# Attention in four phases of sixteen scores a group: four scores copied out by DVE before their exponential, v's sums added up in the SBUF, PSUM banks given out anew in every phase

## The chip, the cores and the metric

The kernel runs on one core of one Trainium2 chip. The metric is device time in microseconds (us) of one execution, as the median of several. One execution is profiled; where a stage is spoken of, its times are counted from the start of the profiled span.

## What is computed

The input x has 2048 tokens of 512 channels. The result mixes a softmax attention with 32 heads of 16 channels and a token-mixing MLP by a gate for each token:

```
qkv    = x @ wqkv                                  # 32 heads, Dh = 16
scores = einsum("bhqd,bhkd->bhqk", q, k) * Dh**-0.5
a      = (softmax(scores) @ v) @ wo
u      = gelu(einsum("bsd,sf->bdf", layernorm(x), w1) + b1)
b      = transpose(einsum("bdf,fs->bds", u, w2) + b2)
out    = g * a + (1 - g) * b                       # g = sigmoid((x * gate_w).sum(-1))
```

## The kernel before

Before the stage that is changed, q, k and v are projected, the layer norm and the first MLP layer are done, and the parts of q and k lie in DRAM (`qp`, `kp`). The changed stage is a hand-written order for all engines: 32 groups (`NG`), each of two heads and one half of the 2048 queries. A group has 64 scores. A score (L806) is one matmul of 128 keys by 512 queries for one head; it uses 64 of the 128 rows of TensorE (`ROWS`, `HALF`), so that it can run beside another matmul of 64 rows. What runs beside the scores is the dense work: the second MLP layer (`second_layer`, tile `dn`) and the output projection (`project`), each matmul done as two halves of 64 rows (L846), the first half in an even phase and the second half in the odd one after it. `put`, `put_outputs` and `sizes_of` write down how many dense matmuls go into which pair of phases (`dense`), and `call` at which pair a transfer is started.

A group runs in eleven phases: ten of six scores and one of four. After the scores of a phase comes `apply_v` for the scores of the phase before: for each score four matmuls (two halves of the queries on two of the four 32-column blocks of TensorE, L770), with 17 columns of v (16 channels and a one, whose product is the softmax's sum). They add up over the whole group in one PSUM bank, `av`.

The PSUM has eight banks: six for scores (`ps_s`, three tiles `s` of two banks), one for `dn`, one for `av`. ScalarE takes two scores in one exponential of 128 x 1024 (L815) from a tile `s` to a tile `pt` in the SBUF, which v's matmuls read.

At the end of a group `evacuate` copies `av` to `ot` (L733), stores the 64 rows of sums (L739, to `o_d`), inverts the softmax's sums on a whole 128 x 512 tile (L743, L744) and stores the inverses a phase later (L749, to `r_d`). Four groups make a block of 128 channels; `fetch_o` brings the block back, with each inverse broadcast over 16 rows (L606, L607), and multiplies and splits it on VectorE (L610, L65, L66: `divide`), when the list `slow` comes to it: at most one such step in an odd phase.

DMAs of this stage are issued by SP in program order: `load_q` of the next group (8 transfers) and `load_k` (6 transfers of 128 KB) at the group's first two phases, the weights of the second layer (L133), stores and fetches between them. A small POOL memset (`token`, L850) orders the two halves of the dense matmuls. After the last group the last block is finished in PSUM (`others`, `last_pair`): the last eight output tiles have then had 8 of their 12 matmuls (`EARLY`).

## Time and profile before

| what | us |
|---|---|
| median of 3 runs | 1308.75 (1307.37 to 1309.79) |
| profiled execution, its span | 1307.9 |
| first stage, to the first exponential | 0 to 304.8 |
| attention, first to last exponential | 304.8 to 1288.2 |
| what follows | 1288.2 to 1307.9 |

The profiled execution's span runs from its first to its last instruction; its own time lies within the runs shown, and the median is 0.85 us above the span. In the lines of the profile below an engine is PE (TensorE's matmuls), PEld (its weight loads), DVE (VectorE), ACT (ScalarE), POOL (GpSimd) or SP (whose queue, SPq, issues DMAs). A row of the timeline has the start, the duration, the engine, the line, the operation and the tiles (out<-in); "x8" are eight of them in a row, and in brackets stands how long the engine was idle before and who released it. A group's row has busy time, mean ns of one, and the idle time before.

### The profile page before, as it was taken

The numbers are of one execution on the slowest core, as the hardware profiler recorded it, in microseconds if no ns is written. First come the engines' busy times: TensorE is split into PE (matmuls) and PEld (weight loads), VectorE is DVE, ScalarE is ACT, GpSimd is POOL, SyncE is SP. The second block draws the span as 40 slices with busy tenths as digits, with TensorE's granted clock in tenths as the row PEclk, the third lists the DMA queues.
The fourth block names the chain that finished last, engine by engine and source line by source line (L and its number), as shares of the span: only waits on it lengthen the run. The fifth ranks groups of instructions, "written<-read, shape, count | busy, mean of one in ns | idle before, by whom it ended". The sixth has DMA issues, their size and how long they took to land.

```text
span 1307.9 us, 32289 instructions
## 1 busy us (share of the span) xinstructions
PE 1299.0 (99%) x13282; PEld 764.0 (58%) x13282; DVE 402.9 (31%) x538; ACT 1090.6 (83%) x1248; POOL 200.9 (15%) x467
## 2 busy tenths in 40 slices
PE   9999999999999999999999999999999999999997
PEld 7888888886555555555555555455555545544444
DVE  5675361445121111122322111232111112233324
ACT  3443343448999999999999999999999999999994
POOL 0210244453101011011100111100010101100000
PEclk9999999999999999999999999999999999999999
DMA  4497643327343334334554343544333333365511
GB/s 129 137 314 274 227 119 98 97 81 154 74 86 66 62 74 84 69 75 92 124 113 120 81 82 73 115 112 118 78 66 62 76 64 78 76 120 120 117 55 69
DMA packets 93384, 138.41 MB, mean 106 GB/s; under 512 B 14293, under 2 KB 53355, under 8 KB 90156
## 3 DMA queue, kind: packets, MB, share of 16 engines
q1 hardware_dynamic: 92652, 135.20, 43.3%
q8 instruction: 107, 1.75, 0.6%
q10 hardware_dynamic: 576, 1.05, 0.2%
q14 instruction: 49, 0.40, 0.1%
HBM read 99.63 MB, written 36.56 MB: 104 GB/s over the span
## 4 chain that ended last, share of the span: by engine, by line
PE 99%; DMA 0%; SPq 0%; DVE 0%; issue 0%
PE av L770 37%; PE s L806 29%; PE acc L414 12%; PE acc L73 10%; PE dn L846 10%; PE pa L889 1%; PE acc L186 1%; PE dn L791 0%; DMA x<-in_A_x_dram 0%; PE acc L253 0%; PE pa L919 0%; SPq L178 0%; DVE base L932 0%; PE pa L897 0%; PE pa L896 0%; SPq L171 0%
## 5 line engine op out<-in xcount | busy, mean ns | idle before, releaser
L815 ACT ACTIVATE pt<-s 128x1024 f32<-128x1024 f32 x1024 | 962.5, 1025 | 20.8 <-PE s L806 13.5
L806 PE MATMUL s<-qs,ks 64*128 64x512 f32 x2048 | 521.2, 420 | 0.0
L770 PE MATMUL av<-pt,v 128*17 128x256 f32 x8192 | 510.6, 381 | 0.0
L806 PEld LDWEIGHTS s<-qs,ks 64*128 64x128 f32 x2048 | 297.6, 184 | 207.7 <-ACT pt L815 183.2
L770 PEld LDWEIGHTS av<-pt,v 128*17 128x17 f32 x8192 | 205.3, 97 | 259.5 <-issue 119.2
L846 PE MATMUL dn<-u_hi,w_hi 64*128 64x512 f32 x428 | 179.7, 420 | 0.0
L846 PE MATMUL dn<-u_lo,w_hi 64*128 64x512 f32 x430 | 170.1, 396 | 0.0
L846 PE MATMUL dn<-u_hi,w_lo 64*128 64x512 f32 x430 | 170.1, 396 | 0.0
L66 POOL TENSOR_TENSOR w_lo<-w_raw,w_hi 128x512 fp32r<-128x512 f32 (+1 forms) x126 | 152.3, 1210 | 115.0 <-ACT w_hi L65 108.4
L850 POOL MEMSET token<- 1x1 f32 x320 | 30.1, 94 | 872.3 <-PE dn L846 695.1
L733 DVE COPY ot<-av 128x512 f32<-128x512 f32 x31 | 21.4, 692 | 347.6 <-PE av L770 347.6
L65 ACT CAST w_hi<-w_raw 128x512 fp32r<-128x512 f32 (+1 forms) x67 | 38.1, 569 | 79.5 <-PE acc L414 58.8
L744 DVE RECIPROCAL rt<-rt 128x512 f32<-128x512 f32 x31 | 104.0, 3353 | 1.1
L414 PE MATMUL acc<-h_hi,w_hi 128*128 128x512 f32 x224 | 87.1, 389 | 0.0
L414 PE MATMUL acc<-h_lo,w_hi 128*128 128x512 f32 x224 | 87.1, 389 | 0.0
L414 PE MATMUL acc<-h_hi,w_lo 128*128 128x512 f32 x224 | 87.1, 389 | 0.0
L65 DVE CAST w_hi<-w_raw 128x512 fp32r<-128x512 f32 (+1 forms) x61 | 23.5, 386 | 190.5 <-PE s L806 82.0
L846 PEld LDWEIGHTS dn<-u_lo,w_hi 64*128 64x128 f32 x430 | 79.5, 185 | 2.5 <-POOL token L850 0.2
L846 PEld LDWEIGHTS dn<-u_hi,w_lo 64*128 64x128 f32 x430 | 79.4, 185 | 2.6
L846 PEld LDWEIGHTS dn<-u_hi,w_hi 64*128 64x128 f32 x428 | 78.8, 184 | 2.2
L73 PE MATMUL acc<-xt_hi,wc_hi 128*128 128x512 f32 x128 | 49.8, 389 | 0.0
L73 PE MATMUL acc<-xt_lo,wc_hi 128*128 128x512 f32 x128 | 49.8, 389 | 0.0
(142 smaller groups left out, 1000.5 us busy)
## 6 DMA issues: line engine op xcount, KB each, us to landing
w_raw<-in_B_w_dram SPq DMA_DIRECT2D x96, 256.0 KB
ks<-kp SPq DMA_DIRECT2D x192, 128.0 KB
qs<-qp SPq DMA_DIRECT2D x256, 64.0 KB
qp<-pc SPq DMA_DIRECT2D x16, 768.0 KB
x<-in_A_x_dram SPq DMA_DIRECT2D x32, 256.0 KB
kp<-pc SPq DMA_DIRECT2D x16, 512.0 KB
w_raw<-in_B_w_dram SPq DMA_DIRECT2D x32, 128.0 KB
bp<-row SPq DMA_DIRECT2D x16, 256.0 KB
```

What stands on the lines that cost most here:

```text
L65: copy(hi, src)
L66: return sub(lo, src, hi.bitcast(F32), ALU.subtract)
L73: nc.tensor.matmul(ps, a, b, start=start and n == 0, stop=stop and n == last)
L186: nc.tensor.transpose(turns[t][:, k, :], xs[t][:, k * P : (k + 1) * P], ident)
L414: nc.tensor.matmul(p, a, b, start=first and k == 0, stop=last and k == 2)
L733: nc.vector.tensor_copy(ot, av)
L744: nc.vector.reciprocal(rt, rt)
L770: nc.tensor.matmul(av[32 * j : 32 * j + VC, i * QC : (i + 1) * QC], v[:, c, g % NP * 2 + i, :], pt[:, h * QC : (h + 1) * QC], start=added[ ...
L806: nc.tensor.matmul(s[:, m, :], kt[grp][rows, c * P : (c + 1) * P], qt[grp][rows, qb * NB : (qb + 1) * NB], start=True, stop=True,)
L815: nc.scalar.activation(pt, s, AF.Exp, scale=SCALE)
L846: mm = nc.tensor.matmul(ps, a[half], b[half], start=first and not second, stop=last and bool(second))
L850: fence = nc.gpsimd.memset(token, 0.0)
```

## The change

A group now runs in four phases of sixteen scores (`PHASES`, `NSC`), 128 phases in all, numbered p. In an even phase 14 dense first halves run beside the scores, in the odd phase after it the 14 second halves. In each phase:

- the scores 1, 3, 5 and 7 are copied by DVE to the SBUF (`EVAC`), and ACT makes one exponential of 128 x 2048 of the four, in place, after all others of the phase (two of 128 x 1024 in the last phase);
- the scores 0, 2, 4, 6, 8 and 9 have an exponential of 128 x 512 each (`SINGLE`), the last six go in pairs (`TWO`; in the first phase of a group the first of these pairs is two single ones);
- seven banks are given out anew (`shares`): scores 0 to 6 take one each, 7 to 9 those of 0 to 2, 10 to 15 those of 3 to 8, and v's matmuls take that of 2 and 9. The bank in which the sums were is the last one that the next phase uses (for its score 6);
- `apply_v` runs in the phase itself, without the four copied scores, which are held back for the next phase (`HELD`). Its sums are closed in every phase, and DVE copies them to `ot` or adds them there. v's weights are 32 columns wide (`v_flat`, of which 17 count). In the first phase of a group the held scores of the group before come first, in a bank of their own, and `store` follows.

`store` writes sums and softmax sums as they are (8 transfers). `invert` fetches the softmax sums of a finished block in the phase after, as a 128 x 64 tile, inverts them and puts them back to `ri_d` in the next one. `fetch_o` has its DVE steps at fixed phases (`on_dve`). The dense work has another order: the second layer first (phases 0 to 91), four phases without dense work, then the output tiles; there is no store and reload of half-made output tiles any more, and of the last eight tiles two have 6 and six have 8 of their 12 matmuls before the end.

```
-    v = v_pool.tile([P, NS, H, VC], F32, name="v")
+    v_flat = v_pool.tile([P, NS * H * VC + HALF], F32, name="v")
+    v = v_flat[:, : NS * H * VC].rearrange("p (t h c) -> p t h c", h=H, c=VC)
...
+        nc.gpsimd.memset(v_flat[:, NS * H * VC :], 0.0)
...
+    PHASES, NSC, BANKS = 4, 16, 7
+    LAST = NG * PHASES - 1
...
+    ri_d = [[dram.tile([P // DH, QW], F32, name=f"ri{h}{k}") for k in range(ND)] for h in range(2)]
...
-    ptp = ptp_ctx.enter_context(tc.tile_pool(name="pt", bufs=6, reuse_waits="tile"))
+    ptp = ptp_ctx.enter_context(tc.tile_pool(name="pt", bufs=2, reuse_waits="tile"))
...
-    ps_s = psum_ctx.enter_context(tc.tile_pool(name="ps_s", bufs=3, space=PSUM, reuse_waits="tile"))
...
-    ps_av = psum_ctx.enter_context(tc.tile_pool(name="ps_av", bufs=1, space=PSUM, reuse_waits="tile"))
...
+    def invert(half, k, pairs, at):
...
+        w = QW // DH
+        t = out_pool.tile([P, w], F32, name="inv")[: n * DH]
+        nc.sync.dma_start(t, r_d[half][k][:n].rearrange("r (a b) -> (r a) b", b=w))
+
+        def turn():
+            nc.vector.tensor_scalar_max(t, t, LEAST_SUM)
+            nc.vector.reciprocal(t, t)
+
+        on_dve(at, turn)
+        def put_back():
+            nc.sync.dma_start(ri_d[half][k][:n].rearrange("r (a b) -> (r a) b", b=w), t)
+
+        calls.setdefault(at + 1, []).insert(0, (put_back,))
...
+    def fetch_o(half, k, places, ats, pairs=4):
...
+        rb = end.tile([P, QW], F32, name="o_sum", bufs=2)[: n * DH]
+        hi, lo = (place(i)[: n * DH] for i in places)
         raw = lo.bitcast(F32)
         nc.sync.dma_start(raw, o_d[half][k][: n * DH])
+        nc.sync.dma_start(rb, ri_d[half][k][:n, None, :].broadcast_to([n, DH, QW]))
+        on_dve(ats[0], nc.vector.tensor_mul, rb, raw, rb)
+        on_dve(ats[1], nc.vector.tensor_copy, hi, rb)
+        on_dve(ats[2], nc.vector.tensor_tensor, lo, rb, hi.bitcast(F32), ALU.subtract)
...
+    def put_output(t, m, at):
+        steps, load = project(t, m)
+        call(2 * at - 2, load)
+        return put(steps, at, [m])
...
+    first, at = steps[:28], put(steps[28:], 0, [14])
+    for t in range(1, NS):
+        at = put(second_layer(t), at, [14] * 3)
+    for half in range(2):
+        for k in range(ND):
+            pairs = 3 if half and k == ND - 1 else 4
+            p0 = PHASES * (half * NP + 4 * k + pairs)
+            call(p0 + 1, invert, half, k, pairs, p0 + 1)
+    p0 = 2 * at
+    call(p0, open_end)
+    call(p0, fetch_o, 0, 0, (0, 1), (p0 + 1, p0 + 1, p0 + 1))
+    call(p0, fetch_o, 0, 1, (2, 3), (p0 + 1, p0 + 2, p0 + 2))
+    call(p0 + 2, fetch_o, 0, 2, (4, 5), (p0 + 2, p0 + 2, p0 + 3))
+    call(p0 + 3, fetch_o, 0, 3, (6, 7), (p0 + 3, p0 + 3, p0 + 3))
+    at += 2
+    for t in range(NH):
+        at = put_output(t, 3 * ND, at)
+    p1 = PHASES * (NP + 2 * 4) + 3
+    call(p1, fetch_o, 1, 0, (8, 9), (p1 + 1, p1 + 2, p1 + 2))
+    call(p1 + 3, fetch_o, 1, 1, (10, 11), (p1 + 4, p1 + 5, p1 + 5))
+    p2 = PHASES * (NP + 3 * 4) + 2
+    assert p2 > 2 * at
+    call(p2, fetch_o, 1, 2, (0, 1), (p2 + 1, p2 + 1, p2 + 1))
+    call(p2 + 4, load_wq, p2 + 4)
+    call(LAST - 1, fetch_o, 1, 3, (2, 3), (LAST, LAST, LAST), 3)
+    for t in range(NH, NS):
+        at = put_output(t, 6 if 2 * at < p2 + 2 else 8, at)
+    assert at == NG * PHASES // 2
...
+    EVAC = 1, 3, 5, 7
+    SINGLE = 0, 2, 4, 6, 8, 9
+    TWO = (10, 11), (12, 13), (14, 15)
+    TURNS = [(0, 2), (4, 6), (8, 9), *TWO]
+    HELD = [(1, 3), (5, 7)]
...
+    def shares(n):
+
+        for one in range(0, BANKS, 2):
+            lows = [k for k in range(one)][::2] + [k for k in range(one + 1, BANKS)][::2]
+            for third in lows:
+                if n in (third, third + 1):
+                    first, second = (low for low in lows if low != third)
+                    return [first, first + 1, one, second, second + 1, 2 * third + 1 - n, n]
+
...
+        for j in range(4):
+            rows, cols = slice(32 * j, 32 * j + VC), slice(j * QC, (j + 1) * QC)
             dst = o_d[half][k][2 * p * DH : 2 * (p + 1) * DH, cols].rearrange("(i r) n -> r i n", i=2)
             nc.sync.dma_start(dst, ot[rows][:DH].rearrange("r (i n) -> r i n", i=2))
-
-        def invert():
-            rt = out_pool.tile([P, NB], F32, name="rt", bufs=1)
-            nc.vector.tensor_scalar_max(rt, ot, LEAST_SUM)
-            nc.vector.reciprocal(rt, rt)
-
-            def store():
-                for rows, cols in blocks:
-                    dst = r_d[half][k][None, 2 * p : 2 * (p + 1), cols]
-                    nc.sync.dma_start(dst, rt[rows][DH:].rearrange("r (i n) -> r i n", i=2))
-
-            stores.append(store)
-
-        slow.insert(0, (two, invert))
-
-    added = [0, 0]
-
-    def pairs_of(g, units, last):
-
-        pairs = list(zip(*([u for u in units if u[2] == qb] for qb in range(2))))
-        return [(g, pair, last and n == len(pairs) - 1) for n, pair in enumerate(pairs)]
-
-    def apply_v(pairs):
-        ot = None
-        for g, pair, last in pairs:
-            for i, c, qb, pt in pair:
-
-                added[qb] += 1
+            dst = r_d[half][k][None, 2 * p : 2 * (p + 1), cols]
+            nc.sync.dma_start(dst, ot[rows][DH:].rearrange("r (i n) -> r i n", i=2))
...
+    def apply_v(av, grp, pairs, final=False):
+
+        for n, pair in enumerate(pairs):
+            for i, c, qb, pt in sorted(pair, key=lambda u: u[2]):
...
+                    v_at = (c * H + grp % NP * 2 + i) * VC
                     nc.tensor.matmul(
-                        av[32 * j : 32 * j + VC, i * QC : (i + 1) * QC],
-                        v[:, c, g % NP * 2 + i, :],
+                        av[32 * j : 32 * (j + 1), i * QC : (i + 1) * QC],
+                        v_flat[:, v_at : v_at + 32],
                         pt[:, h * QC : (h + 1) * QC],
-                        start=added[qb] == 1,
-                        stop=added[qb] == 2 * NS,
+                        start=n == 0,
+                        stop=n == len(pairs) - 1,
...
+        for x, y, more in parts:
+            if more:
+                nc.vector.tensor_tensor(x, y, x, ALU.add)
+            else:
+                nc.vector.tensor_copy(x, y)
+        for n in halves:
+            begun[n] = True
+        if final and grp < NG - 1:
+            store(grp, sums.pop(grp)[0])
...
+        for p in range(LAST + 1):
+            grp, ph = divmod(p, PHASES)
+            second = ph % 2
+            if ph == 0:
+                at = [[0, 0], [0, 0]]
+                if grp + 1 < NG:
                     qt[grp + 1] = load_q(grp + 1)
-                if ph == 1 and grp + 1 < NG:
-                    kt[grp + 1] = load_k(grp + 1)
-                two, second = divmod(ph, 2)
-                two += grp * TWOS
-                if ph == 2 * TWOS:
-                    n_s, beside = 4, []
-                elif second:
-                    n_s = 6
+            if ph == 1 and grp + 1 < NG:
+                kt[grp + 1] = load_k(grp + 1)
+            for what, *args in calls.get(p, ()):
+                what(*args)
+            if not second:
+                beside = [step(*args) for step, *args in dense.get(p // 2, ())]
...
+            head = [second if n < n_b else (n - n_b) % 2 for n in range(NSC)]
...
+                if n < TWO[0][0]:
+                    if n >= BANKS:
+                        ones[share[n - BANKS]] = psum.tile([P, NB], F32, name=f"s{share[n - BANKS]}")
+                    s = ones[share[n % BANKS]]
+                else:
+                    if n == TWO[0][0]:
+                        pool.__exit__(None, None, None)
+                        pool = regions()
+                        psum = pool.__enter__()
+                        twos = {}
+                        for low in range(BANKS):
+                            if low == share[2]:
+                                av = psum.tile([P, NB], F32, name="av")
+                            elif low in share[3:5] and ph == 0:
+                                twos[low] = psum.tile([P, NB], F32, name=f"s{low}")
+                            elif low not in twos:
+                                two = psum.tile([P, 2, NB], F32, name=f"t{low}")
+                                twos[low], twos[low + 1] = two[:, 0, :], two[:, 1, :]
+                                twos[low, low + 1] = two
+                    s = twos[share[(n - BANKS) % BANKS]]
...
+                if n in EVAC:
+                    pt = evac[:, EVAC.index(n), :]
+                    nc.vector.tensor_copy(pt, s)
+                    units[n] = i, c, qb, pt
+                elif n in SINGLE:
+                    pt = ptp.tile([P, NB], F32, name="p1", bufs=len(SINGLE))
+                    nc.scalar.activation(pt, s, AF.Exp, scale=SCALE)
+                    units[n] = i, c, qb, pt
+                else:
+                    units[n] = i, c, qb, None
+                    if n % 2:
+                        pt = ptp.tile([P, 2, NB], F32, name="p2", bufs=len(TWO) + 1)
+                        where = [share[(j - BANKS) % BANKS] for j in (n - 1, n)]
+                        low = min(where)
+                        if (low, low + 1) in twos:
+                            nc.scalar.activation(pt, twos[low, low + 1], AF.Exp, scale=SCALE)
+                        else:
+                            for m in range(2):
+                                nc.scalar.activation(pt[:, m, :], twos[low + m], AF.Exp, scale=SCALE)
+                        for j, k in zip((n - 1, n), where):
+                            units[j] = *units[j][:3], pt[:, k - low, :]
...
+            for x in ([evac] if p < LAST else [evac[:, :2, :], evac[:, 2:, :]]):
+                nc.scalar.activation(x, x, AF.Exp, scale=SCALE)
+            if n_b and second and beside[-1][-1]:
+                beside[-1][-1]()
+            if p == 0:
+                shift_rows(nc.vector, k_bufs[1])
+            if second:
+                for _ in range(2):
                     if len(ready) < 2:
                         split_weight(nc.vector.tensor_copy)
-                    for n, (ready_at, step) in enumerate(slow):
-                        if ready_at <= two:
-                            slow.pop(n)[1]()
-                            break
-
-                n = 2 if ph == 2 * TWOS and grp < NG - 1 else len(late)
-                apply_v(late[:n])
-                late = late[n:] + pairs_of(grp, units, ph == 2 * TWOS)
-        last_ot = apply_v(late)
+            for what, *args in later.get(p, ()):
+                what(*args)
+
+            turns, now_held = ([tuple(units[n] for n in pair) for pair in pairs] for pairs in (TURNS, HELD))
+            spare = share[2]
+            if ph == 0:
+                if held:
+                    apply_v(av, grp - 1, held, final=True)
+                    spare = share[3]
+                    av = psum.tile([P, NB], F32, name=f"s{spare}")
+                whole = {qb for pair in turns for i, _, qb, _ in pair if i}
+                if len(whole) == 1:
+                    now_held = now_held + turns[-1:]
+                    turns = turns[:-1]
+                apply_v(av, grp, turns)
+            elif p < LAST:
+                apply_v(av, grp, held + turns)
+            else:
+                ot = sums[grp][0]
+                nc.vector.tensor_scalar_max(ot, ot, least[0])
+                apply_v(av, grp, held + turns + now_held, final=True)
+                last_ot = ot
+            pool.__exit__(None, None, None)
+            held = now_held
+            if ph == PHASES - 1:
+                assert at == [[NS, NS], [NS, NS]]
...
-                mms = list(enumerate(o_matmuls(1, NH + t, EARLY, 3 * ND)))
+                mms = list(enumerate(o_matmuls(1, NH + t, early[NH + t], 3 * ND)))
...
```

221 lines of the change are left out of this document (82 added, 139 removed).

## The prediction

> **What bounds the kernel now.** First the page's busy times and its chain that ended last, then the stage by itself, then one stretch of the timeline.
>
> ```profile
> span 1307.9 us, 32289 instructions
> PE 1299.0 (99%) x13282; PEld 764.0 (58%) x13282; DVE 402.9 (31%) x538; ACT 1090.6 (83%) x1248; POOL 200.9 (15%) x467
> PE 99%; DMA 0%; SPq 0%; DVE 0%; issue 0%
> ...
> 304.80:1288.20 983.40, 983.40 (x11836) 507.33 (x11832) 227.69 (x240) 962.55 (x1025) 101.06 (x381) 1.00 0.42 87
> ```
>
> The attention lasts 983.4 us. In it PE has no idle time and ACT is busy for 962.6; DVE works 228. Which of the two sets the pace is seen in the steps:
>
> ```profile
> 703.04 0.50 PE L806 MATMUL s<-qs,ks 64*128 64x512 f32 x1
> 703.38 0.39 PE L806 MATMUL s<-qs,ks 64*128 64x512 f32 x1
> 703.61 0.39 PE L806 MATMUL s<-qs,ks 64*128 64x512 f32 x1
> 703.87 7.50 ACT L815 ACTIVATE pt<-s 128x1024 f32<-128x1024 f32 x8 [0.15 <-PE s L806]
> 704.62 1.49 PE L770 MATMUL av<-pt,v 128*17 128x256 f32 x24
> 706.04 0.73 PE L806 MATMUL s<-qs,ks 64*128 64x512 f32 x4
> 706.71 1.06 PE L770 MATMUL av<-pt,v 128*17 128x256 f32 x16
> 707.69 0.49 PE L806 MATMUL s<-qs,ks 64*128 64x512 f32 x1
> ...
> 304.82 5.59 ACT L815 ACTIVATE pt<-s 128x1024 f32<-128x1024 f32 x6
> ...
> L815 ACT ACTIVATE pt<-s 128x1024 f32<-128x1024 f32 x1024 | 962.5, 1025 | 20.8 <-PE s L806 13.5
> ```
>
> PE: six scores, each with a dense matmul, take 1.58 us until v's matmuls start (703.04 to 704.62), two pairs of scores 0.67 (706.04 to 706.71). So a pair costs 0.2275 and a turn to v 0.21. Twenty-four of v's matmuls take 1.42 (704.62 to 706.04), sixteen 0.98: 0.055 each and 0.10 for the turn back. A full phase of six is 3.00 us of PE.
>
> ACT: one exponential lasts 1.025 us, but six run in 5.59 and eight in 7.50, so in a packed row they start every 0.913 or 0.925 us, 0.919 in the mean. Six scores are three of them, 2.76 us, less than PE's 3.00. 1024 x 0.919 = 941 us would do for 983. PE with its eleven pairs of turns a group sets the pace; ACT is only 4% behind it.
>
> **PE's part of the change.** Four pairs of turns a group instead of eleven save 7 x 0.31 = 2.2 us a group, 69 us of PE. A phase of 14 dense matmuls has 15 pairs (14, and the last two scores beside each other): 0.21 + 15 x 0.2275 = 3.62; 64 of v's matmuls 0.10 + 3.52 = 3.62; together 7.24 us, 6.80 in a group's first phase (56 of them) and 7.68 in the second (72).
>
> v's weights with 32 columns instead of 17 cost nothing as long as they load under the matmuls before.
>
> ```profile
> L770 PEld LDWEIGHTS av<-pt,v 128*17 128x17 f32 x8192 | 205.3, 97 | 259.5 <-issue 119.2
> ```
>
> 205.3/8192 = 25 ns of busy load time against 55 ns for each matmul: even at 32/17 of it, 47 ns, they stay under. Uncovered it would be 22 ns x 64 a phase, a case I do not hold likely.
>
> **ACT's part.** ACT gets ten instructions for sixteen scores where it had eight. No exponential of 512 or 2048 is in the trace; the nearest rows are its copies of 512.
>
> ```profile
> 49.85 0.62 ACT L65 CAST wc_hi<-wc_raw 128x512 fp32r<-128x512 f32 x1
> 50.37 0.58 ACT L65 CAST xt_hi<-acc 128x512 fp32r<-128x512 f32 x1
> ...
> 53.65 0.58 ACT L220 COPY v<-acc 128x512 f32<-128x512 f32 x1
> 54.13 0.59 ACT L65 CAST xt_hi<-acc 128x512 fp32r<-128x512 f32 x1
> ```
>
> From a bank 512 elements take a step of 0.48 (53.65 to 54.13), from the SBUF 0.52 (49.85 to 50.37). 512 more elements cost 0.913 - 0.48 = 0.433, so the 2048 take 0.52 + 3 x 0.433 = 1.82. A phase: 6 x 0.48 + 3 x 0.913 + 1.82 = 7.44. With the mean step 0.919 each instruction is 0.006 longer, 7.50: I take that. If every step were as in the stage's mean, 962.5/1024 = 0.940, it would be 0.027 x 10 more, 7.71. A group's first phase splits a pair: 2 x 0.486 - 0.919 = 0.05 more, 1.6 in all. So ACT needs 128 x 7.50 + 1.6 = 961.6 us (953.9 to 988.5): **ACT becomes the bound**, above PE's 7.24. A group's second phase needs 7.68 of PE, 0.18 above ACT, up to 5.8 us over 32 groups; a lead of PE could hide it, but banks bound that lead, so I take 5.
>
> The Trainium skill (ScalarE: Activation LUTs, What ACT_TABLE_LOAD costs) gives 186 ns + 0.833 ns an element less an overlap of about 93 ns, and one element a cycle whatever the function, which speaks against the change: the elements that DVE copies still pass through ACT. By it a phase would be 7.75, ACT's sum 995 and the time, by the sum below, 1356; but it makes the pair 0.946 where the trace packs them at 0.913 to 0.925, so the rows decide.
>
> **DVE's part.** It gets four copies and one addition of 128 x 512 from a bank in each phase, and loses the inversion of whole tiles.
>
> ```profile
> L733 DVE COPY ot<-av 128x512 f32<-128x512 f32 x31 | 21.4, 692 | 347.6 <-PE av L770 347.6
> L744 DVE RECIPROCAL rt<-rt 128x512 f32<-128x512 f32 x31 | 104.0, 3353 | 1.1
> ...
> 86.46 0.68 DVE L357 TENSOR_REDUCE kmax<-acc 128x1 f32<-128x512 f32 x1
> 87.06 0.68 DVE L66 TENSOR_TENSOR pc<-acc,pc 128x512 fp32r<-128x512 f32 x1
> ```
>
> Independent reads of banks start every 0.60 (86.46 to 87.06). Five are 3.1 us of a phase of 7.50, beside work of ACT and PE. But there is a loop through DVE: sums closed, addition 0.60, four copies 2.49, the last two scores that reuse their banks 0.23, turn 0.21, 64 of v's matmuls 3.6, last result 0.3: 7.4, just below ACT. So what holds DVE up ahead of the addition goes into the time almost undiminished, since the addition frees the bank for score 6 and stands ahead of the four copies.
>
> **What holds DVE up: `invert`.** It fetches the softmax sums at the start of a group's second phase, behind `load_k` on SP, and DVE's inversion of them stands ahead of that same phase's addition. Seven of the eight are of this kind (the last has no `load_k` ahead).
>
> ```profile
> 648.17 0.69 DVE L733 COPY ot<-av 128x512 f32<-128x512 f32 x1 [5.12 <-PE av L770]
> 648.89 1.72 SPq L739 DMA_DIRECT2D o<-ot  x4
> 650.66 2.73 SPq L500 DMA_DIRECT2D ks<-kp  x6
> 653.49 0.38 SPq L133 DMA_DIRECT2D w_raw<-in_B_w_dram  x1
> 653.97 2.53 SPq L749 DMA_DIRECT2D r<-rt  x4
> ...
> 653.00:655.00 2.00, 2.00 (x30) 1.02 (x18) 0.34 (x1) 2.00 (x3) 0.00 (x0) 1.00 1.05 123
> 655.00:657.00 2.00, 2.00 (x32) 0.93 (x30) 0.08 (x1) 2.00 (x3) 1.25 (x2) 1.00 0.95 124
> 657.00:659.00 2.00, 2.00 (x30) 1.03 (x30) 0.00 (x0) 2.00 (x3) 0.21 (x2) 1.00 1.06 163
> 659.00:661.00 2.00, 2.00 (x26) 0.94 (x21) 0.05 (x1) 2.00 (x4) 0.00 (x0) 1.00 0.13 45
> ```
>
> Take E as the end of DVE's last addition for the group before, in the first phase: 3.62 for the scores, 0.2 (estimated) until ACT has left the bank of score 9, 16 of v's matmuls 1.06, 0.07 until DVE, 0.69: E is 5.64 after the phase's start. Then SP issues eight stores (1.72 + 2.53, with steps 4.3) and the six of `load_k`. The next to last number of a window is the DMA engines' busy share: after the first of those six (650.66) they are full until 659, some 8.4 us, 8.0 without the weights' 256 KB. A small load behind them lands at about E + 0.05 + 4.3 + 8.0 + 0.3 = E + 12.6. Inverting 64 columns costs 0.6 (64/512 of 3353 ns, and the maximum before). DVE is free for the addition at E + 13.2. It would have been due 7.50 + 3.62 + 0.2 + 4.13 (72 matmuls) + 0.07 = 15.5 after the first phase's start, E + 9.9. Late by 3.3, of which PE's lead with score 6 hides 0.3: 3.0 each, 7 x 3.0 = **21 us**. From below: if the load passed by the others' data, issued at E + 7.1 as it is, and landed within 2 us, nothing; from above, with the full 8.4 and another us of landing, 4.4 x 7 = 31. No row shows a small load behind `load_k`; I take 21, as the full DMA engines are a row.
>
> The Trainium skill (DMA: Bandwidth & Descriptors, Queues, rings and completion order) says that on each DMA engine the descriptors of one issuing queue are consumed in ring order. By that the small load does wait, and 21 stands rather than 0.
>
> **The fetches of the first four blocks** come in the four phases without dense work (92 to 95), all in a row.
>
> ```profile
> 837.57 2.74 SPq L500 DMA_DIRECT2D ks<-kp  x6
> 840.36 0.42 SPq L606 DMA_DIRECT2D o_lo<-o  x1
> 840.82 0.63 SPq L607 DMA_DIRECT2D o_sum<-r  x1
> 851.60 1.23 DVE L610 TENSOR_TENSOR o_sum<-o_lo,o_sum 128x1024 f32<-128x1024 f32 x1 [9.66 <-DMA o_sum<-r]
> 852.86 0.69 DVE L65 CAST o_hi<-o_sum 128x1024 fp32r<-128x1024 f32 x1
> 853.59 1.23 DVE L66 TENSOR_TENSOR o_lo<-o_sum,o_hi 128x1024 fp32r<-128x1024 f32 x1
> ```
>
> `load_k` and one fetch of 1 MB took 14.0 us (837.57 to 851.60), so a queued fetch adds 14.0 - 8.4 = 5.6. Queries (512 KB, estimated at 5 by the 768 KB in 8.0), two fetches, `load_k` (estimated at 7 when queued) and two more fetches: 5 + 11.2 + 7 + 11.2 = 34.4 after phase 92's start, then DVE's three steps 3.2: 37.6. The addition of phase 95 would be due at 3 x 7.50 + 8.0 = 30.5. I take 8, one more for steps that wait in between; 3 if fetches overlap better, 15 if each takes its 11.2 from issue to DVE. The later fetches have a phase or more for themselves and fewer neighbours: nothing.
>
> **The end.** Two tiles have six matmuls left instead of four: 4 x 0.23 = 0.9. The store and reload of half-made tiles saves DMA time that bounds nothing.
>
> **Sum.** 961.6 + 5 + 21 + 8 = 995.6 against 983.4: +12.2, and 0.9: 1307.9 + 13.1 = 1321.0, and 0.85 from span to median: **1322 us**.
>
> **Rivals.** (1) Faster: the small loads are not behind `load_k`'s data. Then ACT alone sets the pace: 961.6 + 5 + 0 + 4 (the fetches queue less too) = 970.6, -12.8 + 0.9, **1297**. For it: each is only 32 KB on engines that also move other transfers. It decides as soon as the sums land 10 us after E. Against: the full windows. (2) The loop through DVE sets the pace. With DVE's reads at their full 0.69 instead of 0.60 and 0.1 more for one hand-over the loop is 7.8: 128 x 7.8 + 21 + 8 = 1027.4, **1354**. For it: the chain 7.4 is only 0.1 below ACT. Against: packed steps of 0.60 are seen. (3) Gain and stalls cancel: half of the 21, no price for the second phases, 980: about **1307**; no mechanism of its own, it is where (1) and the forecast meet.
>
> **Chances.** Forecast 0.57, (1) 0.25, (2) 0.14, (3) 0.04. The range 1286 to 1350: its low end is (1) with ACT's shorter step (7.44, 8 us less) and its high end the forecast with 31 and 15 (+17) and half of ACT's longer step; most of (2) lies beyond. The likeliest case's own range is 1310 to 1345. A difference under 0.2% (2.6 us) can't be told from none here. Faster 0.29 ((1), and a small share of the forecast and (3)), same 0.06, slower 0.65.
>
> **What would show it.** Right: ACT busy without idle in most phases, at about 7.5 us a phase, with exponentials of 512 at steps near 0.49; and seven places, once every four groups, where DVE waits for the transfer into `inv` for 3 us or more, with ACT idle right behind; a longer wait around phases 92 to 95 for `o_sum`. Wrong: no idle time of DVE ahead of the inversions (then (1)); an idle ACT in every phase released by score 14 or 6 (then (2)); PE's busy pairs still at the bound, or v's weight loads over 55 ns each.

## The result, and the profile after

The changed kernel takes 1346.2 us in the median (1344.3 to 1347.4) where the kernel before takes 1308.3: ratio 1.0287, interval 1.0272 to 1.0302, 37.9 us more. The prediction was 1322.

First the head of the changed kernel's page and its chain that ended last; then the attention by itself, and twelve phases without a stall, from the view by windows (columns as in the prediction: PE, PEld, DVE, ACT, POOL busy, granted clock, DMA share, GB/s).

```profile
span 1344.8 us, 33141 instructions
PE 1296.8 (96%) x13278; PEld 850.9 (63%) x13278; DVE 670.2 (50%) x1143; ACT 1094.2 (81%) x1537; POOL 178.6 (13%) x272
...
PE 82%; ACT 7%; DMA 5%; SPq 3%; issue 2%; DVE 1%; DVEq 0%; ACTq 0%
```

```profile
304.80:1325.00 1020.20, 980.87 (x11832) 593.81 (x11832) 494.02 (x844) 966.22 (x1313) 79.00 (x184) 0.98 0.38 80
...
600.00:690.00 90.00, 90.00 (x1116) 55.78 (x1112) 42.61 (x76) 89.52 (x123) 10.16 (x20) 1.00 0.38 76
```

The attention lasts 1020.2 us instead of 983.4, 36.8 more. ACT's work is nearly unchanged (966 against 963), and where nothing stalls ACT is busy for 89.5 of 90 us: that part went as forecast. PE's row is full there as well (90.00), as it was in the kernel before; what sets such a phase is asked by the last two runs below. But over the whole attention ACT is idle for 54 us and PE for 39. The chain now has 5% of DMA and 3% of SP's queue in it, where both stood at 0%.

The length of a phase is read off ACT's timeline, from the start of one exponential of 2048 elements to the next. Four of them in the changed kernel:

```profile
564.30 2.01 ACT L913 ACTIVATE pe<-pe 128x2048 f32<-128x2048 f32 x1
571.68 2.12 ACT L913 ACTIVATE pe<-pe 128x2048 f32<-128x2048 f32 x1
583.04 1.91 ACT L913 ACTIVATE pe<-pe 128x2048 f32<-128x2048 f32 x1
592.07 2.00 ACT L913 ACTIVATE pe<-pe 128x2048 f32<-128x2048 f32 x1
```

The steps are 7.38, 11.36 and 9.03. In a group without a stall they are 7.37, 7.84, 7.49 and 7.54, 30.24 us a group, 967.7 for the 32. Two phases in a row are long here, by 3.5 and by 1.5 us. That pair occurs seven times, this one being a typical one: the seven long phases last 11.0 to 12.9 us and add up to 81.0 (7 x 7.84 would be 54.9), the seven behind them to 62.8 (7 x 7.49 is 52.4).

The place itself, in the changed kernel's timelines of DVE, SP and PE:

```profile
563.32 0.42 DVE L798 TENSOR_TENSOR ot<-av,ot 128x256 f32<-128x256 f32 x1 [1.92 <-PE av L776]
...
576.61 0.19 DVE L618 TENSOR_SCALAR inv<-inv 128x64 f32<-128x64 f32 x1 [7.41 <-DMA inv<-r]
576.84 0.55 DVE L619 RECIPROCAL inv<-inv 128x64 f32<-128x64 f32 x1
577.30 0.36 DVE L798 TENSOR_TENSOR ot<-av,ot 128x256 f32<-128x256 f32 x1
```

```profile
567.98 2.71 SPq L502 DMA_DIRECT2D ks<-kp  x6
570.78 0.37 SPq L615 DMA_DIRECT2D inv<-r  x1
```

```profile
578.14 0.46 PE L876 MATMUL s<-qs,ks 64*128 64x512 f32 x1 [3.15 <-DVE ot L800]
...
581.51 1.86 PE L776 MATMUL av<-pe,v 128*32 128x256 f32 x16
```

E, the end of DVE's last addition for the group before (563.32 + 0.42), is 563.74. The small load is issued at E + 7.0, behind the six of `load_k`, and DVE can invert at E + 12.9; the addition starts at E + 13.6. PE stands still for 3.15 us until the addition frees the bank of score 6. Behind it sixteen of v's matmuls take 1.86 us instead of 1.06, and the view by windows says why:

```profile
576.00:578.00 2.00, 0.00 (x0) 0.00 (x0) 1.36 (x5) 0.00 (x0) 0.00 (x0) 1.00 0.00 0
578.00:580.00 2.00, 1.86 (x13) 1.05 (x14) 2.00 (x4) 1.30 (x3) 0.00 (x0) 0.94 0.51 146
580.00:582.00 2.00, 2.00 (x16) 1.06 (x18) 0.38 (x1) 2.00 (x3) 0.09 (x1) 0.50 0.00 1
582.00:584.00 2.00, 2.00 (x32) 1.01 (x28) 0.00 (x0) 2.00 (x3) 0.00 (x0) 0.71 0.00 0
```

PE's granted clock falls to half after the pause: 0.24 us of the second window, all of the third and 1.16 us of the last, together 3.4 us. The kernel before had a clock of 1.00 in its whole attention.

Two more places, the start (timelines of SP and PE) and phases 92 to 95 (waits of DVE and timeline of ACT):

```profile
296.71 2.64 SPq L502 DMA_DIRECT2D ks<-kp  x6
299.45 6.06 SPq L502 DMA_DIRECT2D qs<-qp  x8
```

```profile
307.23 0.76 PE L876 MATMUL s<-qs,ks 64*128 64x512 f32 x1 [2.56 <-DMA qs<-qp]
```

```profile
DVE o_sum L923 <- DMA o_sum<-ri: 9.2, 1, 9.2
```

```profile
1039.21 1.96 ACT L913 ACTIVATE pe<-pe 128x2048 f32<-128x2048 f32 x1
1048.61 2.00 ACT L913 ACTIVATE pe<-pe 128x2048 f32<-128x2048 f32 x1
1056.01 2.08 ACT L913 ACTIVATE pe<-pe 128x2048 f32<-128x2048 f32 x1
1071.87 1.95 ACT L913 ACTIVATE pe<-pe 128x2048 f32<-128x2048 f32 x1
1080.37 2.01 ACT L913 ACTIVATE pe<-pe 128x2048 f32<-128x2048 f32 x1
```

The four phases take 41.2 us (1039.21 to 1080.37) instead of 30.2. Not all of it is waiting for fetches: the first of the four steps is 9.40 already, 2.0 over the usual 7.37, and DVE waits for no fetch in it. PE works at half clock there (view by windows):

```profile
1037.14:1040.56 3.42, 3.42 (x34) 1.54 (x36) 0.42 (x1) 3.42 (x4) 0.00 (x0) 0.50 0.88 195
```

In four of the kernels below (PE kept busy, and the first three of the parts together) the clock does not fall at this place, and the step is 7.76 or 7.77. So 1.6 us of it are PE's clock. The clock stands at half again behind DVE's long wait, from 1061.0 to 1071.3; what that adds was not measured apart.

The first exponential of the attention starts at 308.03 instead of 304.82.

| Part of the attention | predicted, us | measured, us |
|---|---|---|
| 128 phases without a stall | 966.6 | 967.7 |
| seven stalls at `invert` | 21 | 36.5 |
| the four phases with the fetches of the first four blocks | 8 | 10.9 |
| start | 0 | 5.1 (the rest) |
| sum | 995.6 | 1020.2 |

### The profile page after: what moved, and what is told of

It is laid out like the page before. It is cut to its first block, busy times and chain, and to the rows that moved or that the text cites. A ratio compares the mean times of both kernels' runs of the same rounds, so it can differ in the third digit from the quotient of the medians.

```text
span 1344.8 us, 33141 instructions
## 1 busy us (share of the span) xinstructions
PE 1296.8 (96%) x13278; PEld 850.9 (63%) x13278; DVE 670.2 (50%) x1143; ACT 1094.2 (81%) x1537; POOL 178.6 (13%) x272
## 4 chain that ended last, share of the span: by engine, by line
PE 82%; ACT 7%; DMA 5%; SPq 3%; issue 2%; DVE 1%; DVEq 0%; ACTq 0%
PE av L776 24%; PE s L876 18%; PE acc L416 11%; PE t L876 10%; PE acc L73 9%; PE s L776 4%; DMA inv<-r 3%; PE dn L885 3%; ACT p L897 2%; ACT p L906 2%; ACT pe L913 2%; SPq L502 1%; SPq L767 1%; DMA o_sum<-ri 1%; SPq L765 1%
## 5 line engine op out<-in xcount | busy, mean ns | idle before, releaser
L897 ACT ACTIVATE p<-s 128x512 f32<-128x512 f32 x768 | 397.5, 656 | 54.0 <-PE s L876 29.0
L876 PE MATMUL s<-qs,ks 64*128 64x512 f32 x1344 | 345.5, 408 | 35.3 <-DVE ot L800 17.1
L906 ACT ACTIVATE p<-t 128x1024 f32<-128x1024 f32 x352 | 349.8, 1139 | 0.4 <-PE t L876 0.2
L893 DVE COPY pe<-s 128x512 f32<-128x512 f32 x512 | 317.7, 683 | 6.9 <-PE s L876 6.1
L776 PE MATMUL av<-p,v 128*32 128x256 f32 x4832 | 279.3, 380 | 0.0
L913 ACT ACTIVATE pe<-pe 128x2048 f32<-128x2048 f32 x129 | 260.8, 2024 | 0.0
L776 PEld LDWEIGHTS av<-p,v 128*32 128x32 f32 x4832 | 156.9, 111 | 106.6 <-issue 3.6
L876 PE MATMUL t<-qs,ks 64*128 64x512 f32 x704 | 189.4, 457 | 3.9 <-ACT p L897 0.2
L876 PEld LDWEIGHTS t<-qs,ks 64*128 64x128 f32 x704 | 98.0, 190 | 86.7 <-ACT p L897 78.3
L776 PE MATMUL av<-pe,v 128*32 128x256 f32 x2048 | 144.0, 400 | 0.3 <-ACT pe L913 0.3
L776 PEld LDWEIGHTS av<-pe,v 128*32 128x32 f32 x2048 | 54.9, 112 | 60.7 <-ACT p L897 25.1
```

The costliest lines, as they stand in the source:

```text
L776: nc.tensor.matmul(av[32 * j : 32 * (j + 1), i * QC : (i + 1) * QC], v_flat[:, v_at : v_at + 32], pt[:, h * QC : (h + 1) * QC], start=n == ...
L876: nc.tensor.matmul(s, kt[grp][rows_i, c * P : (c + 1) * P], qt[grp][rows_i, qb * NB : (qb + 1) * NB], start=True, stop=True,)
L893: nc.vector.tensor_copy(pt, s)
L897: nc.scalar.activation(pt, s, AF.Exp, scale=SCALE)
L906: nc.scalar.activation(pt, twos[low, low + 1], AF.Exp, scale=SCALE)
L913: nc.scalar.activation(x, x, AF.Exp, scale=SCALE)
```

## The experiments

All are compared with the kernel before on the same chip (its medians lay between 1308.0 and 1308.5); the differences below are against the 1346.2 of the changed kernel unless another is named.

**The sums' fetch ahead of `load_k`.**

```diff
-            call(p0 + 1, invert, half, k, pairs, p0 + 1)
+            ahead[p0 + 1] = half, k, pairs, p0 + 1
...
+            if p in ahead:
+                invert(*ahead[p])
             if ph == 1 and grp + 1 < NG:
                 kt[grp + 1] = load_k(grp + 1)
```

> The changed kernel, but at the start of a group's second phase the fetch into inv is issued on SP ahead of load_k's six transfers instead of behind them. Theory A (the small load waits behind load_k's data, so DVE's inversion holds the addition): the load is then issued when the sums' stores are done, about 6.3 us after E instead of 7.0, and lands near E + 8.5 instead of E + 12.9, ahead of the addition due at E + 9.7; all seven long phases (11.0 to 11.6 us) and the seven 9.0 us phases behind them go back to 7.8 and 7.5: 7 x 5.1 = 36 us less, about 1310. Theory B (a small load takes that long whatever is ahead of it, by its own round trip behind the stores): DVE waits as before, time within 5 us of 1346.

Measured: 1311.8 us, ratio 1.0027 (1.0017 to 1.0037), 34.5 less. Its timelines of SP and DVE at the same place:

```profile
562.45 0.35 SPq L615 DMA_DIRECT2D inv<-r  x1
562.85 3.86 SPq L502 DMA_DIRECT2D ks<-kp  x6
```

```profile
556.80 0.42 DVE L798 TENSOR_TENSOR ot<-av,ot 128x256 f32<-128x256 f32 x1 [1.92 <-PE av L776]
...
564.26 0.60 DVE L618 TENSOR_SCALAR inv<-inv 128x64 f32<-128x64 f32 x1 [1.58 <-DMA inv<-r]
...
566.96 0.43 DVE L798 TENSOR_TENSOR ot<-av,ot 128x256 f32<-128x256 f32 x1 [1.51 <-PE av L776]
```

E is now 557.22. The load is issued at E + 5.2, has landed at E + 7.0 and the addition at E + 9.7 waits for PE, not for DVE. From issue to use it takes 1.8 us here and 5.8 behind `load_k`'s data. Theory A holds, B falls.

**DVE's inversion one phase later**, SP untouched:

```diff
-            call(p0 + 1, invert, half, k, pairs, p0 + 1)
+            turn_at = p0 + 1 + (pairs == 4 and (half, k) != (1, 2))
+            call(p0 + 1, invert, half, k, pairs, turn_at)
```

> The changed kernel with SP's order untouched; DVE's inversion and the store of its result stand one phase later for six of the seven blocks (not for the seventh, whose fetch follows at once). Theory A: the load has 7.5 us more, DVE finds it landed, six of seven stalls go: 6 x 5.1 = 31 us less, about 1315.5, and the one that stays looks as before. Theory C (the lost time is not DVE's wait but the DMA traffic itself, ks and the sums, slowing the phase): nothing changes, 1346.

Measured: 1316.9, ratio 1.0066 (1.0050 to 1.0081), 29.3 less; the one stall that was left in place is still there (11.1 and 10.4 us, where the changed kernel has 11.0 and 9.4). The load still lands late and does no harm: it is DVE's order that costs, not the traffic. C falls.

**PE kept busy during the wait.**

```diff
+            if pairs == 4:
+                after_turn.add(p0 + 2)
...
+                for _ in range(14 if p in after_turn and n == 5 else 1):
                     nc.tensor.matmul(
```

> The changed kernel; in the seven phases that wait behind the inversion, score 5 is computed fourteen times over instead of once (same operands, same bank), so that PE works for some 3 us while DVE waits. The wait itself stays. Theory D (the 1.5 us lost in the phase after a stall, 9.0 for 7.5, come from PE's clock, granted at 0.50 for 3.4 us after 3.15 us without work): the clock stays at 1.00, the following phases take 7.5 and the whole 7 x 1.5 = 10.7 us less, about 1335.5; the long phases stay at 11.0 or more. Theory E (those 1.5 us are the loop through DVE and the banks catching up after the wait): the following phases stay at 9.0, 1346 or a little more.

Measured: 1339.6, ratio 1.0238 (1.0224 to 1.0252), 6.7 less. The same stall as above, by windows and in the timelines of PE and ACT:

```profile
576.00:578.00 2.00, 1.83 (x11) 1.23 (x11) 1.67 (x5) 0.00 (x0) 0.00 (x0) 1.00 0.01 3
578.00:580.00 2.00, 2.00 (x16) 1.08 (x15) 2.00 (x4) 1.61 (x4) 0.00 (x0) 1.00 0.51 145
580.00:582.00 2.00, 2.00 (x34) 1.05 (x34) 0.07 (x1) 2.00 (x4) 0.09 (x1) 1.00 0.03 8
```

```profile
580.65 1.07 PE L779 MATMUL av<-pe,v 128*32 128x256 f32 x16
```

```profile
571.42 2.10 ACT L917 ACTIVATE pe<-pe 128x2048 f32<-128x2048 f32 x1
582.61 1.94 ACT L917 ACTIVATE pe<-pe 128x2048 f32<-128x2048 f32 x1
590.42 1.99 ACT L917 ACTIVATE pe<-pe 128x2048 f32<-128x2048 f32 x1
```

The long phase stays (11.19), the clock stays at 1.00, sixteen of v's matmuls take 1.07 us again, and the next phase takes 7.81 instead of 9.03. Over all seven, the phases behind the long ones add up to 54.6 us instead of 62.8. So 8.2 of the 10.4 us lost after the waits, four fifths, are PE's clock, as theory D has it. For the last 0.3 us of each theory E, the loop catching up, is left, but nothing shows it. The whole gains less, 6.7, among other things because phases 92 to 95 take 1.3 us more in this run.

**The place of the keys in the SBUF**: the pools of probabilities, operands and outputs opened ahead of that of the output weights.

```diff
-    o_pool = ...
-    stk = ...
-    out_pool = ...
...
-    ptp = ...
...
+    ptp = ...
+    stk = ...
+    out_pool = ...
+    o_pool = ...
```

> The changed kernel with its pools in another order in the SBUF (probabilities, scores' operands, outputs, then the output weights), so that group 0's keys no longer lie where the first layer's last operands are read; their first transfer then stands between the weights' on SP, as in the kernel before. Theory F (the attention starts 3.2 us late and 1.8 more are lost at half clock, because the first keys and queries are issued late): first exponential near 304.8 instead of 308.0, no half clock behind it, 5 us less, about 1341. Rival: the start is late through other work, time unchanged within 1.5 us.

Measured: 1342.4, ratio 1.0265 (1.0247 to 1.0282), 3.8 less. Its timelines of SP and ACT:

```profile
286.69 0.38 SPq L502 DMA_DIRECT2D ks<-kp  x1
```

```profile
305.63 3.05 ACT L895 ACTIVATE p<-s 128x512 f32<-128x512 f32 x6 [1.45 <-PE s L874]
...
311.27 2.02 ACT L911 ACTIVATE pe<-pe 128x2048 f32<-128x2048 f32 x1
```

The first key transfer is ten us earlier, the first six exponentials run packed from 305.63, and the first of 2048 starts at 311.27 instead of 315.55. Most of the loss at the start comes from the memory that the keys inherit: before the change the pool of the output weights held five more buffers of 4 KB a partition, and the operands lay behind them.

**The third fetch early.**

```diff
-    call(p0 + 2, fetch_o, 0, 2, (4, 5), (p0 + 2, p0 + 2, p0 + 3))
-    call(p0 + 3, fetch_o, 0, 3, (6, 7), (p0 + 3, p0 + 3, p0 + 3))
+    call(p0, fetch_o, 0, 2, (4, 5), (p0 + 2, p0 + 3, p0 + 3))
+    call(p0 + 2, fetch_o, 0, 3, (6, 7), (p0 + 3, p0 + 3, p0 + 3))
```

> The changed kernel with a third buffer for o_sum: block 2's fetch is issued with those of blocks 0 and 1 at phase 92's start instead of at phase 94's, block 3's at phase 94's start instead of 95's. Theory G (phases 92 to 95 lose 11 us because the third fetch is issued only when a buffer is free, while the DMA engines stood at a quarter of their time around 1048 us): the wait of 9.2 us ahead of o_sum shrinks to 4 or less, some 5 us less, about 1341. Rival (those four phases hold more bytes than the DMA engines carry in 30 us, and the order changes nothing): within 2 us of 1346.

Measured: 1348.3, ratio 1.0297 (1.0283 to 1.0311). The wait moved from the third fetch to the fourth; the four phases take 41.3 us. Theory G falls.

**No gap between the fetches**: `load_k` and the fourth fetch moved up as well, into a fourth buffer.

> The changed kernel with a different order on SP around phase 92: queries, the fetches of blocks 0, 1 and 2, then group 24's load_k (a phase earlier than elsewhere, ahead of the sums' stores), and block 3's fetch at phase 93's start into a fourth buffer. In the run with the third fetch early the DMA engines stood nearly idle from 1052 to 1056 us, since stores waited on SP behind the fetches and load_k and the fourth fetch behind them; then DVE waited 8.8 us for the fourth. Theory H (the loss of 11 us in phases 92 to 95 is that idle time of the DMA engines, wherever it lies): with 5.9 MB in one row from 1030 at some 190 GB/s the last lands about 1061, DVE's wait is under 3 us, 6 to 9 us less: 1337 to 1340. Rival (the bytes alone need the 41 us): within 2 us of 1346.

Measured: 1347.1, ratio 1.0290 (1.0271 to 1.0309), 42.0 us for the four phases, now spread over all four. This order gains nothing, but it does not refute theory H, since the gap only moved: SP needed 13.98 us to issue the six transfers of `load_k` behind the fetches (2.71 elsewhere), the sums' stores and the fourth fetch came only after that, and from 1056 to 1062 the DMA engines' share is 0.25, 0.14 and 0.11.

**Fewer bytes**, of the divisors in one run and of the results in another.

```diff
-        nc.sync.dma_start(rb, ri_d[half][k][:n, None, :].broadcast_to([n, DH, QW]))
+        nc.sync.dma_start(rb[:, :few], ri_d[half][k][:n, None, :few].broadcast_to([n, DH, few]))
```

In either run the columns that are not fetched are set to one, so these two kernels leave three quarters of the first four blocks undivided, or without their results.

> The changed kernel, but of the first four blocks' divisors only a quarter of the columns is loaded (the rest is set to one on POOL; those outputs stay undivided): four times 128 KB instead of 512 KB into o_sum, 1.5 MB less of some 5.9 MB in phases 92 to 95. Theory I (those phases are as long as their bytes: about 41 us in all three orders of the fetches): 1.5 MB at 190 GB/s are 8 us, so the four phases take about 33 us and the whole about 1338. Rival (the waits come from the order on SP and from when the sums are ready, not from bytes): within 2 us of 1346.

> The counterpart: of the first four blocks' undivided results only a quarter of the columns is loaded (the rest is set to one on POOL), the divisors whole; again 1.5 MB less. Theory I: the same 8 us less, about 1338. If the broadcast of the divisors (64 reads of each row) costs more than its bytes, this run gains less than the one with a quarter of the divisors, by more than 3 us.

Measured: 1335.6 with a quarter of the divisors (ratio 1.0213, 1.0196 to 1.0230), 10.6 less and 31.9 us for the four phases; 1340.2 with a quarter of the results (1.0249, 1.0232 to 1.0267), 6.0 less and 37.0 us. The same bytes gain 4.6 us more where the broadcast is cut (a broadcast in which each row is read 16 times, not 64). While a divisors' fetch runs, the kernel with the third fetch early shows half of the DMA engines at work:

```profile
1046.00:1048.00 2.00, 2.00 (x38) 1.15 (x40) 1.93 (x3) 2.00 (x4) 0.00 (x0) 1.00 0.51 141
...
1050.00:1052.00 2.00, 2.00 (x10) 0.93 (x8) 2.00 (x4) 2.00 (x5) 0.00 (x0) 1.00 0.57 150
```

**Sixteen rows.** Each row of divisors is stored twice, so that the fetch's outermost dimension is 16 instead of 8.

```diff
+            for twin in range(2):
+                dst = ri_d[half][k].rearrange("(r twin) (a b) -> twin r a b", twin=2, b=w)[twin, :n]
+                nc.sync.dma_start(dst, t)
...
-        nc.sync.dma_start(rb, ri_d[half][k][:n, None, :].broadcast_to([n, DH, QW]))
+        nc.sync.dma_start(rb, ri_d[half][k][: 2 * n, None, :].broadcast_to([2 * n, DH // 2, QW]))
```

> The changed kernel; each row of inverted sums is stored twice in the DRAM, so that the fetch of a block's divisors reads 16 rows, each to 8 partitions, instead of 8 rows to 16 partitions each: the same 512 KB into the same place. A quarter of the divisors' bytes was worth 10.6 us, a quarter of the results' 6.0, though the bytes are the same, and while a divisors' fetch runs alone the DMA engines show a busy share near 0.5. Theory J (a transfer whose outermost dimension is 8 runs on 8 of the 16 DMA engines, as the Trainium skill has it in DMA: Bandwidth & Descriptors, Why a DMA increments its semaphore by 16 and not by 1): with 16 rows it runs on all, the share goes to about 1 and the fetches need about half the time for these 2 MB, some 6 us of the 11 are gained: about 1340. Rival (the repeated reading of a row is what costs): within 2 us of 1346.

Measured: 1341.4, ratio 1.0255 (1.0241 to 1.0269), 4.8 less and 35.8 us for the four phases. Theory J holds, and with it the rule of the Trainium skill that the expectation names. Sixteen rows also halve how often a row is read, so the time alone leaves the rival standing; the packets in the traces decide. From 1046 to 1052 us of the kernel with the third fetch early a packet of 4 KB takes 0.21 us in the median, and 8.4 packets are under way at a time in the mean. In this kernel, in the last 3 us of the first two fetches (1038 to 1041), a packet takes 0.24, no less, but 16.3 are under way.

**The parts together.** Without the sixteen rows:

> The sums' fetch ahead of load_k, the third fetch early, and the other order of the pools together. If the three losses are separate: 1346 less 34.5, less 3.8, less some 5: about 1303, below the kernel before (ratio near 0.996). If they overlap (one loss hidden under another): 1308 or more.

> The sums' fetch ahead of load_k, the pools in the other order, and this order of the fetches. With theory H: 1346 less 34.5, less 3.8, less 6 to 9: 1299 to 1302, ratio to the kernel before 0.993 to 0.995. With its rival: 1307.5, as in the run of three parts.

Measured: 1307.5 (ratio 0.9987, 0.9977 to 0.9997) with the third fetch early, 1306.5 (0.9984, 0.9975 to 0.9993) with the other order of fetches. The stalls and the start add up as forecast, the fetches give nothing. With the sixteen rows:

> Sixteen rows together with the sums' fetch ahead of load_k and the pools in the other order. With theory J: 1346 less 34.5, less 3.8, less 6: about 1302, ratio 0.995. With its rival: 1308.

> The same with the third fetch early. If the fetches now end in time for each phase wherever they start, no difference to the run before; if the third was still late through its issue, up to 4 us less: 1298 to 1302.

Measured: 1300.7 (0.9944, 0.9931 to 0.9958), and with the third fetch early 1295.7 (0.9902, 0.9887 to 0.9917). The early third fetch, worth nothing while its divisors ran on half of the engines, is worth 5 us when they don't, and the sixteen rows are worth 11.8 beside it (1307.5 to 1295.7). In the four phases, 31.9 us long here, the windows of this last kernel read:

```profile
1008.00:1010.00 2.00, 2.00 (x42) 0.92 (x34) 0.00 (x0) 0.70 (x1) 0.00 (x0) 1.00 1.02 254
1010.00:1012.00 2.00, 2.00 (x12) 1.16 (x10) 1.92 (x4) 1.47 (x4) 0.00 (x0) 1.00 1.03 258
```

All DMA engines are at work, at 254 and 258 GB/s instead of 141 and 150. This kernel beats both: 12.5 us below the kernel before, 50.5 below the changed one.

**What sets a phase without a stall.** Two runs on the kernel with the sums' fetch ahead (1311.8): DVE's last copy of a phase twice, and ACT's last single exponential twice.

```diff
                     nc.vector.tensor_copy(pt, s)
+                    if n == EVAC[-1]:
+                        nc.vector.tensor_copy(pt, s)
```

> The kernel with the sums' fetch ahead of load_k (1311.8), and DVE makes its last copy of each phase twice (same bank, same place), 0.60 us more of DVE a phase. The prediction's loop through DVE (7.4 us, 0.1 below ACT's phase): 128 x 0.50 = 64 us more, about 1376. Rival (the loop through DVE has more than 0.6 us to spare, or the copy falls into its idle time): within 10 us of 1312.

> The kernel with the sums' fetch ahead of load_k (1311.8), and ACT makes the last single exponential of each phase twice (same bank, same place), 0.48 us more of ACT a phase. ACT as the bound: 128 x 0.48 = 61 us more, about 1373. If another engine or the loop through DVE set the pace, less than half of that.

Measured: 1397.2 with the copy (ratio 1.0677, 1.0661 to 1.0693), 85.4 more, 0.67 a phase; 1384.8 with the exponential (1.0585, 1.0569 to 1.0601), 73.1 more, 0.57 a phase. Timelines, the copy's run first:

```profile
699.50 1.87 DVE L895 COPY pe<-s 128x512 f32<-128x512 f32 x3
701.40 0.69 DVE L897 COPY pe<-s 128x512 f32<-128x512 f32 x1
...
706.85 3.04 ACT L901 ACTIVATE p<-s 128x512 f32<-128x512 f32 x6 [0.63 <-PE s L878]
```

```profile
702.91 3.70 ACT L900 ACTIVATE p<-s 128x512 f32<-128x512 f32 x7
```

The repeated copy follows 0.71 us behind its twin, which writes the same place (699.50 + 1.87 - 0.68 is the third copy's start, 700.69). Of 0.71 us, 0.67 reach the time: the loop through DVE has nothing to spare, and ACT now waits 0.63 us for a score. Seven exponentials take 3.70 where six take 3.05; of these 0.65 us 0.57 arrive, so about 0.1 us was to spare there in a phase. Between 600 and 900 us PE is busy for all 300 us before either edit, for 278.6 with the copy and for 282.3 with the exponential: its full row did not mean that PE sets the pace. But the repeated exponential is that of score 9, whose bank v's matmuls take next, so it delays the loop through DVE as well. These two runs do not tell a bound of ACT alone from that loop.

## Why the prediction was wrong, point by point

**The sign and the mechanism were right.** A phase is no longer set by PE and takes about 7.5 us, with single exponentials at steps of 0.48 as forecast, and the change pays once every four groups at `invert`, because the small load stands behind `load_k`'s data. A phase without a stall takes 7.56 us in the mean against 7.55 (966.6/128). Which of the two bounds it is stays open: the prediction had the loop through DVE at 7.4 and ACT at 7.5, and nearly all of either repeat reaches the time, 0.67 of 0.71 and 0.57 of 0.65. The loop that rival (2) names is thus at the phase's length, or within 0.1 of it; its 7.8 is wrong. v's weights of 32 columns cost nothing: sixteen of v's matmuls last 1.07 us at full clock, 1.06 before.

**The step that failed is the sum's term for the stalls: "3.0 each, 7 x 3.0 = 21 us".** It measured 5.2 each, 36.5. The landing was forecast at E + 12.6 and came to use at E + 12.9, the addition at E + 13.6 instead of E + 13.2, against E + 9.7 when due: the long phase by itself costs 3.7 in the mean (26.1/7). The rest, 1.5 us each, was not in the sum at all, nor in its upper bound: PE stands still for 3.15 us and then works at half clock for 3.4. With PE kept busy 1.2 of the 1.5 went. The prediction's row of the attention has a clock of 1.00, in a stage in which PE has no idle time, and the prediction did not ask what the stall that it forecast would do to that clock.

**"I take 8" for the fetches measured 10.9**, of which 1.6 are the half clock in the first of the four phases, again not in the sum. The rows it was built from were right (a fetch of 1 MB behind another transfer in 5.6 us), but they were of the kernel before, where one fetch ran beside the reads of `load_k`. Four in a row are limited by the divisors' broadcast, which ran on half of the DMA engines: with sixteen rows and the third fetch early the four phases last 31.9, and little more than what the first of them loses is left.

**The start has no term in the sum and cost 5.1**, of which another order of the pools gave 3.8 back. The pool of the output weights had become smaller, and the keys took over other memory. That could be seen in the change, not in the trace before: a prediction has to ask what a change moves in memory, too. The end's 0.9 did not show: the tail behind the attention lasts 19.8 us against 19.7.

Rival (1), 1297 us, describes the kernel that the experiments arrived at (1295.7), but for another reason than it gave: the small load does wait behind `load_k`, and had to be moved. That the two numbers are close is luck.

The ends of the range are added up a little wrong: (1) less 8 is 1289 and not 1286, and 1322 with 17 and half of ACT's longer step (13) is 1352 and not 1350. Nothing hangs on it.

## What to carry to other kernels

A load of a few KB that an engine waits for in order belongs ahead of the large transfers of its queue, or its consumer a phase later; either cost one moved line here and gave 29 to 35 us. A stall of PE of some 3 us is to be priced with the time at half clock behind it, here 3.7 and 1.5. Where a broadcast feeds the path, look at the DMA share while it runs alone: near 0.5 meant half of the engines here, and neither of the two other orders of the fetches helped until its outermost dimension was 16.

## What the runs showed of the hardware

PE's clock: 3.15 us without work were enough for the granted clock to fall to 0.50, for 3.4 us, and it fell only when PE was at work again. The Trainium skill (TensorE: Matmul & The Clock Gate, Part 1: The HAM clock gate) has half rate after an idle window of about 3.4 us that runs freely; the trace agrees with the half and the length. It does not agree that the window has to be idle: in the attention of all runs each spell of half clock lasts 3.4 us or a multiple of it, and in the 3.4 us ahead of this one PE was busy for 1.62 (first line below).

DMA engines: the Trainium skill (DMA: Bandwidth & Descriptors, Why a DMA increments its semaphore by 16 and not by 1) says that a transfer issued this way uses the largest number of engines, up to 16, that divides the outermost dimensions of both sides. The trace agrees: share 0.51 to 0.57 with 8 rows, 1.02 and 1.03 with 16.

One kind of drop comes without any long pause. In the last kernel, at the first of the phases without dense work, PE's longest pause is 0.34 us (its timeline), and still the clock falls. The windows are the 3.4 us ahead of a drop: at the stall in the changed kernel, at phase 92 in the changed kernel, and at phase 92 in the last kernel, with the half clock behind it.

```profile
1002.42 1.09 PE L878 MATMUL s<-qs,ks 64*128 64x512 f32 x4 [0.34 <-DVE pe L895]
```

```profile
576.35:579.76 3.41, 1.62 (x12) 0.95 (x12) 3.12 (x8) 1.06 (x3) 0.00 (x0) 1.00 0.24 69
...
1033.73:1037.14 3.41, 2.68 (x12) 1.14 (x10) 2.83 (x8) 3.40 (x8) 0.00 (x0) 1.00 0.73 199
```

```profile
1000.99:1004.40 3.41, 2.69 (x14) 1.08 (x10) 3.10 (x9) 3.40 (x8) 0.00 (x0) 1.00 0.68 209
1004.40:1007.81 3.41, 3.41 (x30) 1.52 (x34) 0.42 (x1) 3.41 (x5) 0.00 (x0) 0.50 0.88 261
```

The phase takes 9.4 us. What the three have in common is few matmuls, 12 to 14 in 3.4 us, where the 3.4 us ahead of the third line have 62. In the traces of all runs here each fall from full clock in the attention follows such a stretch, in which at most 14 matmuls began; but not each such stretch is followed by a fall, and no run changed this number alone, so the rule behind it stays open. In the kernel of three parts the clock stayed at 1.00 at the same place.
